# Dividing the streamed weight loads of a SwiGLU kernel at other feature tiles

**Chip, core, metric.** The kernel runs on one core of a Trainium2 chip. The metric is the device time of one execution in microseconds. The profile's span, which excludes launch work, is shorter by some 1.8 us (82.74 us against a span of 80.96 for the profiled execution of the kernel before).

## The reference

```python
# x: 32 x 32 x 512, w1 and w3: 512 x 1792, w2: 1792 x 512, all bf16
gate = einsum("bsd,df->bsf", x, w1)
up   = einsum("bsd,df->bsf", x, w3)
h    = silu(gate) * up
out  = einsum("bsf,fd->bsd", h, w2)
```

There are 1,024 rows of x, and 1,792 features are 14 "feature tiles" of 128.

## The kernel before

All weights fit on chip; the art is to start before they are there. The loads run in this order, all but two (`nc.scalar`) on the queue of SyncE:

```python
FK = 3
# ... (load_x and load_w, each one dma_start)
load_x(nc.sync, 0, 1)
load_x(nc.scalar, 1, 2)
load_w(nc.sync, w1_sb, w1_v, 0, FK, 0, 2)      # first group: tiles 0 to 2, in halves of the contraction
nc.scalar.activation(table[:], one, SIGMOID)
load_w(nc.scalar, w1_sb, w1_v, 0, FK, 2, DT)
load_w(nc.sync, w3_sb, w3_v, 0, FK, 0, 2)
load_w(nc.sync, w3_sb, w3_v, 0, FK, 2, DT)
nc.sync.dma_start_transpose(out=xT[:, :, HB:NB], in_=x_flat[HB:NB, :])
for c0, c1 in ((FK, 7), (7, 10), (10, FT)):    # three pairs of loads: w1 then w3
    load_w(nc.sync, w1_sb, w1_v, c0, c1)
    load_w(nc.sync, w3_sb, w3_v, c0, c1)
nc.sync.dma_start_transpose(out=xT[:, :, NB:N], in_=x_flat[NB:N, :])
nc.sync.dma_start(out=w2_sb[:], in_=w2_v)
```

TensorE warms up, turns the first 256 rows of x, and projects tiles 0 to 2 for those rows, then for the next 256 (its "second half"), then tiles 3 to 13 for all 512 rows:

```python
keep_warm(6, NB)                  # six matmuls on constants while x is on its way
# ... x turned; first halves of tiles 0 to 2: twelve gate, then twelve up matmuls of 256 columns
for fo in range(FK):              # second halves
    project(gates[fo], w1_sb, fo, HB, NB, range(DT), HB)
    project(ups[fo], w3_sb, fo, HB, NB, range(DT), HB)
    swiglu(gates[fo], ups[fo], fo, 0)
for nb in range(NBLK):            # two blocks of 512 rows
    for fo in range(FK if nb == 0 else 0, FT):
        # gate: four matmuls of 512 columns; up: four; then swiglu on ScalarE and VectorE
        ...
# ... then out = h w2, by 128 rows
```

Tile 3 is thus the first to need a load of the three pairs.

## Time and profile before

| | kernel before |
|---|---|
| time, median of the first 3 runs | 83.0 us (82.97 to 83.38) |
| span of the profiled execution | 80.96 us |
| TensorE busy | 94% of the span |
| VectorE / ScalarE busy | 49% / 29% |
| granted TensorE clock | 1.00 |

TensorE bounds the kernel; the prediction shows the lines. One more view of this kernel matters below, the timeline of TensorE's first group (start, length, engine, line, work, count):

```profile
4.78 1.48 PE L121 MATMUL gate_ps<-xT,w_sb 128*128 128x256 bf16 x12
6.10 1.47 PE L121 MATMUL up_ps<-xT,w_sb 128*128 128x256 bf16 x12
```

Twelve matmuls take 6.10 - 4.78 = 1.32 us from first start to next start, 0.11 us each.

### The profile page before, as it was taken

Reading aid. Unit: us, or ns where it says so; the run is one execution under the profiler, and the core shown is the slowest. Engines: PE = TensorE matmul, PEld = TensorE weight load, DVE = VectorE, ACT = ScalarE, POOL = GpSimd, SP = SyncE. Lnnn points to the kernel's source line nnn. Section 1 sums busy time; section 2 is a strip of 40 time slices with the busy share of each in tenths; the row PEclk is TensorE's granted clock in tenths of the full one; section 3 lists DMA queues with packets and bytes.
Section 4 is the critical chain, followed back from the end, with each engine's and each line's share of the span. In section 5 each row is a group of like instructions: output and inputs, shape, how many; then the busy total and the mean of one; then the engine's idle time right before and its main releaser. Section 6 shows DMA issues by size and latency. Waiting matters only on the chain.

```text
span 81.0 us, 1014 instructions
## 1 busy us (share of the span) xinstructions
PE 76.5 (94%) x382; PEld 37.4 (46%) x388; DVE 39.7 (49%) x60; ACT 23.4 (29%) x40; POOL 0.7 (1%) x6
## 2 busy tenths in 40 slices
PE   6999979999999999999999999999999999999960
PEld 2378824444444444444444444444444444444540
DVE  0040698887887887877887877873000000000010
ACT  4330742222343222343222443220220220220220
POOL 3000000000000000000000000000000000000000
DMA  1999999999992000000000000000011011011012
GB/s 10 311 284 269 349 336 344 222 67 291 350 350 64 0 0 0 0 0 0 4 8 0 0 0 0 4 0 0 15 50 65 24 41 65 29 44 65 27 41 62
DMA packets 10789, 7.67 MB, mean 95 GB/s; under 512 B 3616, under 2 KB 10784, under 8 KB 10784
## 3 DMA queue, kind: packets, MB, share of 16 engines
q1 hardware_dynamic: 10368, 7.28, 33.9%
q10 hardware_dynamic: 416, 0.33, 1.2%
q8 instruction: 3, 0.05, 0.2%
q14 instruction: 2, 0.02, 0.1%
HBM read 5.77 MB, written 1.05 MB: 84 GB/s over the span
## 4 chain that ended last, share of the span: by engine, by line
PE 82%; DMA 9%; SPq 4%; issue 1%; DVE 0%; DVEq 0%
PE o_ps L174 30%; PE up_ps L121 27%; PE gate_ps L121 26%; DMA w_sb<-in_w_dram 9%; SPq L66 2%; SPq L78 2%; SPq L62 0%; DVE o_sb L183 0%; DVEq L183 0%
## 5 line engine op out<-in xcount | busy, mean ns | idle before, releaser
L121 PEld LDWEIGHTS <-w_sb 128*128 128x128 bf16 x248 | 24.0, 98 | 25.1 <-DMA w_sb<-in_w_dram 1.5
L121 PE MATMUL up_ps<-xT,w_sb 128*128 128x512 bf16 (+1 forms) x122 | 28.7, 358 | 0.5 <-DMA w_sb<-in_w_dram 0.4
L121 PE MATMUL gate_ps<-xT,w_sb 128*128 128x512 bf16 (+1 forms) x122 | 28.7, 358 | 0.3
L131 ACT ACTIVATE sig<-gate_ps 128x512 f32<-128x512 f32 x28 | 16.7, 597 | 32.2 <-PE gate_ps L121 32.2
L174 PE MATMUL o_ps<-w_sb,hT 128*128 128x512 bf16 (+2 forms) x124 | 24.3, 355 | 0.1
L133 DVE TENSOR_TENSOR t<-gate_ps,sig 128x512 f32<-128x512 f32 x28 | 19.3, 690 | 9.0 <-ACT sig L131 8.9
L134 DVE TENSOR_TENSOR hT<-t,up_ps 128x512 bf16<-128x512 f32 x28 | 19.3, 688 | 2.9
L174 PEld LDWEIGHTS <-hT 128*128 128x128 bf16 x126 | 11.8, 98 | 12.7
L183 DVE CAST o_sb<-o_ps 128x128 bf16<-128x128 f32 x1 | 0.3, 291 | 23.0 <-PE o_ps L174 23.0
L185 ACT CAST o_sb<-o_ps 128x512 bf16<-128x512 f32 (+1 forms) x8 | 4.6, 572 | 19.6 <-PE o_ps L174 19.6
L92 PE MATMUL warm_ps<-const-bfloat16-1.0 128*128 128x512 bf16 x6 | 2.7, 623 | 0.8 <-PEq L205 0.8
L114 DVE CAST xT<-pT 128x256 bf16<-128x256 f32 (+1 forms) x3 | 1.1, 380 | 4.0 <-PE pT L104 3.9
L74 ACT ACT_TABLE_LOAD x1 | 1.3, 1283 | 1.2 <-PEq L205 1.2
L92 PEld LDWEIGHTS <-const-bfloat16-1.0 128*128 128x128 bf16 x6 | 0.7, 133 | 1.9 <-issue 1.9
L104 PEld LDWEIGHTS <-x_sb 128*128 128x128 bf16 x8 | 0.8, 135 | 1.0 <-DMA x_sb<-in_x_dram 1.0
L104 PE MATMUL pT<-ident,x_sb 128*128 128x128 bf16 x8 | 1.1, 308 | 0.1
L114 ACT CAST xT<-pT 128x128 bf16<-128x128 f32 (+1 forms) x2 | 0.6, 320 | 1.6 <-PE pT L104 1.6
masks.py:199 POOL TENSOR_SCALAR_AFFINE_SELECT ident<-ident 128x128 bf16<-128x128 bf16 x1 | 0.3, 292 | 0.1
masks.py:197 POOL MEMSET ident<- 128x128 bf16 x1 | 0.2, 204 | 0.3 <-POOLq L205 0.3
L74 ACT ACTIVATE table<-const-bfloat16-1.0 128x1 f32<-128x1 bf16 x1 | 0.2, 202 | 0.0
L205 POOL MEMSET const-bfloat16-1.0<- 128x1 bf16 x1 | 0.1, 101 | 0.0
L205 POOL MEMSET const-uint8-127<- 128x1 uint8 x1 | 0.1, 101 | 0.0
(2 smaller groups left out, 0.2 us busy)
## 6 DMA issues: line engine op xcount, KB each, us to landing
w_sb<-in_w_dram SPq DMA_DIRECT2D x4, 512.0 KB, 7.5
w_sb<-in_w_dram SPq DMA_DIRECT2D x1, 1792.0 KB, 8.6
out_dram<-o_sb SPq DMA_DIRECT2D x7, 128.0 KB, 1.7
w_sb<-in_w_dram SPq DMA_DIRECT2D x2, 384.0 KB, 7.8
w_sb<-in_w_dram SPq DMA_DIRECT2D x3, 192.0 KB, 3.9
w_sb<-in_w_dram ACTq DMA_DIRECT2D x1, 192.0 KB, 3.7
x_sb<-in_x_dram ACTq DMA_DIRECT2D x1, 128.0 KB, 3.0
x_sb<-in_x_dram SPq DMA_DIRECT2D x1, 128.0 KB, 2.8
```

What stands on the lines that cost most here:

```text
L66: queue.dma_start(out=w_sb[:, d0:d1, f0:f1], in_=w_v[:, d0:d1, f0:f1])
L74: nc.scalar.activation(table[:], one, SIGMOID)
L78: nc.sync.dma_start_transpose(out=xT[:, :, HB:NB], in_=x_flat[HB:NB, :])
L92: nc.tensor.matmul(warm_ps[:, 0:cols], lhsT=one.to_broadcast([P, P]), rhs=one.to_broadcast([P, cols]), start=True, stop=True,)
L104: nc.tensor.matmul(pT[:, i, j, :], lhsT=x_sb[:, nt, dt * P : (dt + 1) * P], rhs=ident[:], start=True, stop=True,)
L114: copy(xT[:, dts[0] : dts[-1] + 1, nts[0] * P : (nts[-1] + 1) * P], pT[:].rearrange("p d t c -> p d (t c)"),)
L121: nc.tensor.matmul(ps[:, c0 : c0 + n1 - n0], lhsT=w_sb[:, dt, fo * P : (fo + 1) * P], rhs=xT[:, dt, n0:n1], start=(dt == 0), stop=(dt == D ...
L131: nc.scalar.activation(sig[:], gate_ps[:], SIGMOID)
L133: nc.vector.tensor_mul(t[:], gate_ps[:], sig[:])
L134: nc.vector.tensor_mul(hT[:, fo, nb * NB : (nb + 1) * NB], t[:], up_ps[:])
L174: nc.tensor.matmul(o_ps[:], lhsT=hT[:, fo, nt * P : (nt + 1) * P], rhs=w2_sb[:, fo, c0 : c0 + DB], start=(fo == 0), stop=(fo == FT - 1),)
L185: nc.scalar.copy(o_sb[:], o_ps[:])
```

## The change

The intent: the first pair carries only tiles 3 to 5, so that it lands sooner; tile 6 moves to the second pair. Count, order and total bytes of the loads stay.

```diff
-    for c0, c1 in ((FK, 7), (7, 10), (10, FT)):
+    for c0, c1 in ((FK, 2 * FK), (2 * FK, 10), (10, FT)):
         load_w(nc.sync, w1_sb, w1_v, c0, c1)
         load_w(nc.sync, w3_sb, w3_v, c0, c1)
```

## The prediction

> **What bounds the kernel now.** I read four views of the kernel before, each to narrow the question. First the busy shares and the chain that ended last, to see which engine sets the end:
>
> ```profile
> PE 76.5 (94%) x382; PEld 37.4 (46%) x388; DVE 39.7 (49%) x60; ACT 23.4 (29%) x40; POOL 0.7 (1%) x6
> ...
> PE 82%; DMA 9%; SPq 4%; issue 1%; DVE 0%; DVEq 0%
> ```
>
> TensorE is busy for 94% of an 81.0 us span. It makes up 82% of the chain; one weight transfer makes up 9%. So a change of transfers is worth only what TensorE idles for them. The chain in order of time (start, length, what) shows where TensorE takes over:
>
> ```profile
> 4.64 6.89 DMA w_sb<-in_w_dram
> 11.53 0.05 issue
> 11.58 1.04 PE up_ps L121 x4
> 12.62 0.86 PE gate_ps L121 x4
> ```
>
> From 11.58 us to the last output the chain is TensorE almost without a break. What starts it is one load issued at 4.64 us that lands at 4.64 + 6.89 = 11.53 us. By the order of issue in the code this is w3 of feature tiles 3 to 6, the second load that the change touches. The timeline around that moment (start, length, engine, line, work, in brackets the idle time before):
>
> ```profile
> 9.60 0.60 PE L121 MATMUL up_ps<-xT,w_sb 128*128 128x256 bf16 x4
> ...
> 10.09 0.55 PEld L121 LDWEIGHTS <-w_sb 128*128 128x128 bf16 x4 [0.17 <-DMA w_sb<-in_w_dram]
> 10.32 0.81 PE L121 MATMUL gate_ps<-xT,w_sb 128*128 128x512 bf16 x3
> ...
> 11.57 24.50 PEld L121 LDWEIGHTS <-w_sb 128*128 128x128 bf16 x115 [0.94 <-DMA w_sb<-in_w_dram]
> 11.58 1.04 PE L121 MATMUL up_ps<-xT,w_sb 128*128 128x512 bf16 x4 [0.45 <-DMA w_sb<-in_w_dram]
> ```
>
> The bracketed numbers are not the loss: weight loads run ahead of the matmuls, and the end of a matmul is modelled. I take the loss from starts. The groups of four 256-column matmuls start at 7.41, 7.85, 8.29, 8.72, 9.16 and 9.60 us, 0.435 us apart, so tile 3's gate could have started at 9.60 + 0.435 = 10.04 us. Later groups of four 512-column matmuls start every 0.865 us (12.45, 13.31, 14.18), 0.216 us each. One of the gate's four records is missing (x3, the first shown at 10.32), so I choose to put its true start one matmul earlier, at 10.10 us, which fits the weight load at 10.09. The gate ends at 10.10 + 0.865 = 10.97 us, and the up projection starts at 11.58. **Loss at the first wait 10.10 - 10.04 = 0.06 us, at the second 11.58 - 10.97 = 0.61 us, together 0.67 us.** The sum of waits lists only three weight-load waits on these transfers (1.5 us); the third is 0.38 us before the first projection at 4.78 us and lies before anything that changes.
>
> Last, the view of the weight loads, one issue at a time (durations of the issue, then its start, then the time to landing), for the two loads that are waited for:
>
> ```profile
> L66 SPq DMA_DIRECT2D w_sb<-in_w_dram x1: 575/575/575, 4.0 to 4.0; - x1
> DMA to landing us min/median/max: 6.0/6.0/6.0
> ...
> L66 SPq DMA_DIRECT2D w_sb<-in_w_dram x1: 505/505/505, 4.6 to 4.6; - x1
> DMA to landing us min/median/max: 6.9/6.9/6.9
> ```
>
> So w1 of tiles 3 to 6 lands at 4.02 + 6.0 = 10.0 to 10.05 us, w3 at 11.53. Asked in the same way, the other four (issued at 5.19, 5.92, 6.51, 8.84) have 7.6, 8.0, 8.9 and 8.0 us to landing: w1 and w3 of tiles 7 to 9 land at 12.8 and 13.9 us, w1 and w3 of tiles 10 to 13 at 15.4 and 16.8. The spacing is 1.48, 1.27, 1.1, 1.5 and 1.4 us: about 1.45 us for 512 KB and 1.2 us for 384 KB. All six were issued by 8.84 us and the stretches from 8 to 15 us move 333 to 357 GB/s each, so a transfer lands when the bytes ahead of it have gone through; its own issue time hardly matters.
>
> **What the Trainium skill says.** "DMA: Bandwidth & Descriptors", section "Why a DMA increments its semaphore by 16 and not by 1": only the full count means that all data has landed. So tile 3, one quarter of the 512 KB, can't be used before the load of all four tiles is complete. The trace agrees: the gate's weight load starts at 10.09, right after the landing. "Perfetto Trace Analysis", section "DMA Optimizations", says that splitting transfers "may allow some to start sooner"; here the count of transfers stays and only a boundary moves, but the reason is the same. The first page's section "Specifications" asks for at least 512 B for line rate; the pieces become 3 x 128 x 2 B = 768 B instead of 1,024 B in the first pair, and the two 384 KB loads of before, whose pieces are also 768 B, took 1.27 and 1.1 us, that is 310 and 357 GB/s, against 354 for the first 512 KB, so I see no clear penalty. "TensorE: Matmul & The Clock Gate", section "Back-to-back issue gap", has 518 cycles for 512 columns (216 ns at its 2.4 GHz) beside a sustained figure of 131 ns; the trace has 216 ns, so no faster pace is to be had here and only idle time can be won.
>
> **The change part by part.** No instruction is added or removed: six loads, the same bytes, the same order, no change in the compute code. The sizes go from 512, 512, 384, 384, 512, 512 KB to 384, 384, 512, 512, 512, 512 KB.
>
> 1. w1 of the first pair carries 128 KB less. At 345 GB/s (mean of the stretch) that is 131,072 B / 345 = 0.38 us, so it lands at about 9.65 us, before TensorE wants it at 10.04. The first wait (0.06 us) goes.
> 2. w3 of the first pair has 256 KB fewer ahead of and in it: 0.76 us earlier by bytes, 11.53 - 0.76 = 10.77 us. By spacings (9.65 plus 1.1 to 1.27) it is 10.75 to 10.92 us. From landing to matmul took 0.05 us before, so the earliest start is 10.80 to 10.97. TensorE gets there at 10.04 + 0.865 = 10.90 us. So 0 to 0.07 us of wait remains, and the up projection starts at 10.90 to 10.97 instead of 11.58: 0.61 to 0.68 us gained.
> 3. Tile 6 moves into the second pair. It is wanted at 10.04 + 3 x 1.73 = 15.2 us (gate) and 16.1 us (up). Ten tile-loads of 128 KB are then done instead of eleven at w1's landing, so it lands at about 12.8 - 0.4 = 12.4 us; w3 completes the same fourteen as before and lands at 13.9. That leaves 2.8 and 2.2 us.
> 4. Tiles 10 to 13 land as before, at 15.4 and 16.8 us, and are wanted from 10.04 + 7 x 1.73 = 22.1 us on. The transposed x and w2 come behind the same bytes.
>
> Sum: 0.67 us less a remnant of some 0.05: about 0.62 us. It is all on the path, as TensorE runs without a stop from 11.58 us on. I let 0.6 stand: span 81.0 to 80.4, time 83.0 to 82.4 us.
>
> **Rivals.** (a) *The gain is eaten by VectorE or PSUM.* VectorE works almost without a pause from 8.68 to about 17.3 us on a backlog, and TensorE runs closer behind it now. If it blocked TensorE, nothing would be won: 83.0. Against it: a tile costs VectorE 0.69 + 0.69 us against 1.73 on TensorE, and with four buffers per tag, tile 4's up projection (12.63 after the change) needs tile 0's product, which ended at 10.17, 2.4 us before; that margin grows from tile to tile. I give it 3%.
> (b) *The first load does not shrink in proportion*, because of shorter pieces or because landing is mostly fixed latency. If both loads take the slower 1.27 us and w1 lands only 0.2 us earlier, w3 lands at 11.1 us; a wait of 0.25 us remains, the gain is 0.4 us and the time 82.6. Some 20%.
> (c) *The second pair becomes the wait.* It would have to slip by over 2.2 us; nothing in the steady rate speaks for that. Below 2%; then 83 or more.
> (d) *The gain drowns in the spread.* The three runs before are 82.97, 83.00 and 83.38, and the profiled one 82.74: a spread as large as the gain. The trace will show it anyway; the median may be off by 0.2.
>
> **Range and chances.** Even all idle time removed is 0.67 / 83.0 = 0.8%, so over 2% (below 81.3 us) has no source; 2% slower (above 84.7 us) needs a new wait of 1.7 us, of which I find none. The range goes from a full gain on a quick run (82.0) to almost no visible gain (82.9).
>
> **What would show it.** Right: the up projection of tile 3 starts at 10.9 to 11.0 us; no weight-load wait ahead of tile 3's gate that costs TensorE a start; no wait before tile 6 near 15.2 us; matmul pace unchanged at 0.216 us; every later start, and the end of the span, 0.6 us earlier. Wrong: w3 of the first pair landing after 11.1 us (rival b), a new gap near 15.2 or 16.1 us (c), or an early gain that is gone again before the output stage at 54.05 us (a).

## The result, and the profile after

| session | before: median, runs | after: median, runs | ratio, 95% interval |
|---|---|---|---|
| first | 83.31 us, 6 (one slow) | 81.97 us, 6 | 0.987 (0.982 to 0.992) |
| second | 82.92 us, 11 | 82.37 us, 6 | 0.993 (0.988 to 0.999) |
| third | 82.89 us, 11 | 82.15 us, 6 | 0.992 (0.987 to 0.997) |

A ratio is the mean time of one kernel's fast runs over that of the other's in the same rounds, so it is not quite the ratio of the medians quoted. The differences of the means of fast runs are 1.08, 0.60 and 0.61 us. The change is faster by 0.7 to 1.3%.

The profiled execution of the changed kernel, however, shows almost none of this: it took 82.69 us against 82.74, a span of 80.9 us against 80.96. First its busy times and its chain, by engine:

```profile
PE 77.1 (95%) x382; PEld 37.9 (47%) x388; DVE 39.5 (49%) x60; ACT 23.4 (29%) x40; POOL 0.7 (1%) x6
...
PE 95%; issue 1%; DVE 0%; DVEq 0%
```

The weight transfer (9% before) is gone from the chain: TensorE alone sets the end, from the first warming matmul on. The loads did come sooner; this is the view of the two first loads after (issue's duration and start, then time to landing):

```profile
L66 SPq DMA_DIRECT2D w_sb<-in_w_dram x1: 576/576/576, 4.0 to 4.0; - x1
DMA to landing us min/median/max: 5.4/5.4/5.4
...
L66 SPq DMA_DIRECT2D w_sb<-in_w_dram x1: 505/505/505, 4.6 to 4.6; - x1
DMA to landing us min/median/max: 6.0/6.0/6.0
```

6.0 and 6.9 us became 5.4 and 6.0 us: w1 lands at 9.4 us, w3 at 10.65 instead of 11.53. But the timeline shows TensorE coming later:

```profile
4.60 2.31 PE L121 MATMUL gate_ps<-xT,w_sb 128*128 128x256 bf16 x12
6.75 1.47 PE L121 MATMUL up_ps<-xT,w_sb 128*128 128x256 bf16 x12
...
10.24 0.60 PE L121 MATMUL up_ps<-xT,w_sb 128*128 128x256 bf16 x4
...
10.89 0.81 PE L121 MATMUL gate_ps<-xT,w_sb 128*128 128x512 bf16 x3
...
11.54 1.03 PE L121 MATMUL up_ps<-xT,w_sb 128*128 128x512 bf16 x4
```

The same twelve gate matmuls took 6.75 - 4.60 = 2.15 us instead of 1.32. Their starts in the trace are 0.213 us apart at first and 0.109 us at the end, twice the pace from some point on. Eight of the twelve were slow, so the clock was released at about 4.60 + 8 x 0.213 = 6.3 us. In the profile before it had been released by 4.78. This one accident of the execution cost 0.83 us (0.18 of it won back, as the group began at 4.60 instead of 4.78), and put TensorE at tile 3's up projection at 10.24 + 0.435 + 0.865 = 11.54 us, long after w3 was there. No idle time stands in the line at 11.54: the wait is gone, and the time it would have saved was used up ahead of it. The profile prints the granted clock as 1.00 for this execution too; the slow start is to be seen only in the pace of the matmuls.

That splits the question in two. Theory A: the change does nothing but remove TensorE's wait for w3; what that is worth differs from execution to execution. Theory B: most of the measured gain is a chance mixture of early and late clocks.

### The profile page after: what moved, and what is told of

Read it like the earlier page. It is cut to its first block, busy times and chain, and to the rows that moved or that the text cites. A ratio compares the mean times of both kernels' runs of the same rounds, so it can differ in the third digit from the quotient of the medians.

```text
span 80.9 us, 1014 instructions
## 1 busy us (share of the span) xinstructions
PE 77.1 (95%) x382; PEld 37.9 (47%) x388; DVE 39.5 (49%) x60; ACT 23.4 (29%) x40; POOL 0.7 (1%) x6
## 4 chain that ended last, share of the span: by engine, by line
PE 95%; issue 1%; DVE 0%; DVEq 0%
PE gate_ps L121 31%; PE o_ps L174 30%; PE up_ps L121 30%; PE warm_ps L92 3%; PE pT L104 1%; DVE o_sb L183 0%; DVEq L183 0%
## 5 line engine op out<-in xcount | busy, mean ns | idle before, releaser
L121 PEld LDWEIGHTS <-w_sb 128*128 128x128 bf16 x248 | 24.6, 100 | 24.6 <-DMA w_sb<-in_w_dram 0.3
L121 PE MATMUL gate_ps<-xT,w_sb 128*128 128x512 bf16 (+1 forms) x122 | 29.5, 368 | 0.2
```

The costliest lines, as they stand in the source:

```text
L121: nc.tensor.matmul(ps[:, c0 : c0 + n1 - n0], lhsT=w_sb[:, dt, fo * P : (fo + 1) * P], rhs=xT[:, dt, n0:n1], start=(dt == 0), stop=(dt == D ...
```

## The experiments

Twelve kernels ran in three further sessions of four, each beside runs of the kernel before; the second and third rows above are from the first and the last of them. One number orders all of them. From the start of tile 3's up projection TensorE runs to the end without a stop, so the span is that start plus a constant. "TensorE ready" is worked out from the starts, as in the prediction: the start of tile 2's last up group + 0.435 + 0.865 us. "Middle" and "last" are the mean of the eighth and ninth, and the last, of the sixteen part completions that the trace records for w3 of the first pair; the last one is the landing. (They are read from the semaphore events in the trace files; no view prints the middle ones.)

| execution profiled | TensorE ready | w3 middle | w3 last | up of tile 3 starts | span |
|---|---|---|---|---|---|
| before | 10.90 | 9.91 | 11.53 | 11.58 | 81.0 |
| null_before | 10.93 | 10.01 | 11.22 | 11.26 | 80.6 |
| after | 11.54 | 9.00 | 10.65 | 11.54 | 80.9 |
| same_after | 11.16 | 10.00 | 10.22 | 11.16 | 80.5 |
| after_again | 11.67 | 9.21 | 11.02 | 11.67 | 81.0 |
| w1_only | 10.54 | 9.52 | 11.39 | 11.44 | 80.8 |
| first5 | 11.13 | 11.20 | 11.67 | 11.72 | 81.1 |
| first2 | 11.53 | 9.33 | 9.50 | 11.53 | 80.9 |
| cold_before | 12.27 | 10.19 | 11.39 | 12.27 | 81.6 |
| cold_after | 12.87 | 9.30 | 10.72 | 12.87 | 82.2 |
| plain_before | 11.14 | 9.56 | 10.77 | 11.14 | 80.5 |
| plain_after | 11.35 | 9.08 | 10.16 | 11.35 | 80.7 |

In all twelve the start is the later of two times, "TensorE ready", and "w3 last" plus 0.04 to 0.05 us; and the span is the start plus 69.3 to 69.4 us. (The two probes, which move work, have another constant.)

### The two kernels again: null_before, same_after, after_again

No edit: the kernel before, and the changed kernel twice.

> The kernel before, unchanged, timed against itself, and a second profile of it. Theory A (the whole gain is TensorE's removed wait for w3 of the first pair; in the first profile it was 0.67 us, and the further 0.4 to 0.5 us of the measured gain come from executions in which that load lands later than in the profiled one): ratio 1.000 within 0.003, and in the new profile the up projection of tile 3 again starts only after w3's landing, at 11.6 to 12.1 us. Theory B (the measured gain is mostly a mixture of executions whose TensorE clock was released early or late in the first 7 us; the loads move little): ratio 1.00 but with single runs falling into two groups some 0.8 us apart, and no wait much over 0.6 us.

Measured: 82.52 us, ratio 0.997 (0.990 to 1.004). The single runs spread from 82.15 to 83.31 us, those of the kernel before beside them from 82.39 to 83.57. The timeline of this second profile of the kernel before:

```profile
9.63 0.60 PE L121 MATMUL up_ps<-xT,w_sb 128*128 128x256 bf16 x4
...
11.26 1.04 PE L121 MATMUL up_ps<-xT,w_sb 128*128 128x512 bf16 x4 [0.17 <-DMA w_sb<-in_w_dram]
```

TensorE was ready at 9.63 + 0.435 + 0.865 = 10.93 us and waited 0.33 us; w3 landed 0.31 us sooner than in the first profile. The expectation of theory A (a start of 11.6 us or later) failed in its number: the two profiles of this kernel have waits of 0.68 and 0.33 us.

> The changed kernel again, for a second profile and a tighter ratio. Theory A: ratio 0.987 to 0.992; in a profile with the clock released before the first projection (first group of gate matmuls 1.3 us from first to last start, not 2.15) tile 3's up projection starts at 10.8 to 11.0 us with no wait, span near 80.1. Theory B: ratio above 0.995 once ten more runs are in, and the spans of single runs in two groups 0.8 us apart as wide as those of the kernel before.

Measured: 82.37 us, ratio 0.993 (0.988 to 0.999), between what theory A (at most 0.992) and theory B (above 0.995) had named.

```profile
9.86 0.60 PE L121 MATMUL up_ps<-xT,w_sb 128*128 128x256 bf16 x4
...
10.51 0.81 PE L121 MATMUL gate_ps<-xT,w_sb 128*128 128x512 bf16 x3
11.16 1.03 PE L121 MATMUL up_ps<-xT,w_sb 128*128 128x512 bf16 x4
```

There is no wait at tile 3, as expected, but the start is 11.16, not 10.8 to 11.0. The clock was released in time here; instead the second halves began late, because the transposed x landed only at 7.64 us. Its span is 80.5 us, not 80.1: again the start plus the constant.

> The changed kernel a third time, for the comparison with the two-tile version on one chip and for another profile: ratio to the kernel before 0.987 to 0.994, span of the profiled run equal to the start of tile 3's up projection plus 69.4 us within 0.05 us.

Measured: 82.15 us, ratio 0.992 (0.987 to 0.997); start 11.67, span 81.0, as expected. This third profile has the latest clock of the three (2.38 us for the first twelve matmuls, from 4.49 to 6.87). What follows: the changed kernel did not wait for w3 in any of its three profiles, whatever delayed TensorE. The single runs of the changed kernel spread nearly as widely in these two sessions (81.82 to 82.86 us) as those of the kernel before (82.36 to 83.57). Theory B's two groups are half there: in the second session five runs of the kernel before lie at 82.39 to 82.63 us, five at 83.17 to 83.57 and one between, but in the third they are spread evenly, and the changed kernel's runs form no groups. In all three sessions the interval of the ratio lies below 1, so a chance mixture of clocks, theory B, is an unlikely source of the gain.

### Half the change, and the opposite: w1_only, first5

```diff
-    for c0, c1 in ((FK, 7), (7, 10), (10, FT)):
-        load_w(nc.sync, w1_sb, w1_v, c0, c1)
+    for (a0, a1), (c0, c1) in (((FK, 6), (FK, 7)), ((6, 10), (7, 10)), ((10, FT), (10, FT))):
+        load_w(nc.sync, w1_sb, w1_v, a0, a1)
         load_w(nc.sync, w3_sb, w3_v, c0, c1)
```

> Half of the change: only w1's boundary moves to 3 to 5 and 6 to 9, w3 keeps 3 to 6 and 7 to 9. w3 of the first pair then has 128 KB fewer ahead of it instead of 256 KB: it lands 0.38 us earlier instead of 0.76. Theory A: part of the gain, 0.35 to 0.45 us, ratio 0.994 to 0.996, with a wait of 0.2 to 0.4 us left ahead of tile 3's up projection. Theory B, or a gain that comes from w1's own wait (0.06 us in the trace): ratio either 1.00 or the full 0.987.

Measured: 82.50 us, ratio 0.994 (0.988 to 1.000), as theory A said; by the means it gains 0.51 us, a little more than the 0.35 to 0.45 expected. It lies between the kernel before and the changed one (0.993 on the same chip, in the same rounds) and is told apart from neither. Its profile has the earliest TensorE of all and the longest wait:

```profile
9.24 0.60 PE L121 MATMUL up_ps<-xT,w_sb 128*128 128x256 bf16 x4
...
11.44 1.04 PE L121 MATMUL up_ps<-xT,w_sb 128*128 128x512 bf16 x4 [0.66 <-DMA w_sb<-in_w_dram]
```

It was ready at 10.54 us and waited 0.90 us, not the 0.2 to 0.4 expected: w3's middle part came at 9.52 us, 0.39 us sooner than the 9.91 of the first profile, as the bytes say, but the last part lagged 1.87 us behind it.

```diff
-    for c0, c1 in ((FK, 7), (7, 10), (10, FT)):
+    for c0, c1 in ((FK, 8), (8, 11), (11, FT)):
```

> The opposite dose: the first pair covers five tiles (3 to 7), then 8 to 10, then 11 to 13. w1 lands 128 KB / 345 GB/s = 0.38 us later than in the kernel before, w3 0.76 us later. Theory A: the wait grows one for one, up projection of tile 3 at about 12.3 us, span and time 0.7 to 0.8 us longer than before, ratio 1.008 to 1.010. Theory B: ratio within 0.003 of 1.

Measured: 83.60 us, ratio 1.008 (1.001 to 1.014), one run slow; the means give 83.52 - 82.93 = 0.59 us longer.

```profile
11.72 1.04 PE L121 MATMUL up_ps<-xT,w_sb 128*128 128x512 bf16 x4 [0.42 <-DMA w_sb<-in_w_dram]
```

The sign and, nearly, the size are theory A's (0.7 to 0.8 us was expected); the interval excludes 1, though not the upper end of theory B's range (1.003). In the profile the start is 11.72 and not 12.3, since the lag was only 0.47 us in that execution, while the middle part came at 11.20 us, later by 1.29 us than in the first profile. Of that, 0.54 us was there before the pairs began: the transposing load ahead of them landed at 7.61 instead of 7.07 us. The other 0.75 us is what the bytes say.

### The landing by itself: probe_before, probe_after

Tile 3's projections are put ahead of the second halves of tiles 1 and 2; the result is the same. The second probe has the changed boundaries. The diff is shortened; the loop over the remaining tiles then begins at tile 4.

```diff
-    for fo in range(FK):
-        (second half of fo)
+    (second half of tile 0)
+    (gate, up and swiglu of tile 3)
+    for fo in range(1, FK):
+        (second half of fo)
```

> A probe of the landing by itself: boundaries of the kernel before, but tile 3's projections stand ahead of the second-half projections of tiles 1 and 2 (same work, same result), so TensorE gets to tile 3's up projection 1.74 us earlier, at about 9 us, and always waits for w3, whatever its clock did. The time is then w3's landing plus a constant. Expected: a wait of some 2.3 us ahead of tile 3's up projection, time 1.7 us over the kernel before, that is about 84.4 to 84.8 us, ratio 1.02. If the landing itself scatters from execution to execution (theory A), the single runs scatter by 0.5 us or more; if the scatter of the kernel before comes from TensorE's clock (theory B), they lie within 0.2 us.

> The same probe with the changed boundaries. The difference of the two probes is the mean shift of w3's landing over many executions. By bytes (256 KB at 345 GB/s) the load lands 0.76 us earlier: 83.7 to 84.0 us, ratio to the other probe 0.991. Theory A as first stated (landings late in unprofiled executions make the larger gain): a shift of 1.0 us or more.

Measured: 83.97 us, ratio 1.008 (1.002 to 1.014), and 83.90 us, ratio 1.008 (1.003 to 1.013). The first probe's line and then, in its own fence, the second's:

```profile
10.96 1.04 PE L121 MATMUL up_ps<-xT,w_sb 128*128 128x512 bf16 x4 [0.50 <-DMA w_sb<-in_w_dram]
```

```profile
11.04 1.04 PE L121 MATMUL up_ps<-xT,w_sb 128*128 128x512 bf16 x4 [0.27 <-DMA w_sb<-in_w_dram]
```

Neither the 1.7 us over the kernel before (the means give 0.62) nor the wait of 2.3 us came true. Without a wait TensorE would have been ready for the up projection at 9.55 and 9.18 us; part of the waiting fell ahead of the gate, which had to wait for w1 until 9.42 and 9.73 us, and w3 came earlier than in the first profile. In these two executions w3 landed at 10.91 us with the old boundaries and at 10.99 with the new. The middle parts came at 10.20 and 9.19 us, but the lags were 0.71 and 1.81 us and hid the difference. The expected shift of 0.76 us (a ratio of 0.991 between the probes) did not show: the fast runs have means of 83.78 and 83.76 us. Two of the six runs of the first probe, 84.89 and 86.36 us, count as slow and are left out, and that decides the result: with them its mean is 84.40 us. So the pair neither confirms nor measures the mean shift.

What it does show is the scatter. TensorE waits for w3 in both profiles, so the time is the landing plus a constant, and the fast runs still lie 83.59 to 84.07 and 83.14 to 84.05 us: the landing itself differs by 0.5 to 0.9 us between executions. If the two slow runs keep the constant (span minus 71.1 us in the profiled execution), w3 landed there at about 12 and 13.5 us; no trace of them was kept, and the second had a granted clock of 0.98, so that its constant may have been longer.

### TensorE late on purpose: cold_before, cold_after

```diff
-    keep_warm(6, NB)
+    keep_warm(1, NB)
```

> The kernel before with one warming matmul in place of six, so that TensorE is still at its slow pace (0.21 us for 256 columns in place of 0.11) through the first group and gets to tile 3 later than w3 lands. Theory A and B agree that the time rises, by 0.5 to 2 us. In the trace there should be no wait ahead of tile 3's up projection.

> The changed kernel with one warming matmul. If the change does nothing but bring w3 forward, it is worth nothing where TensorE comes later than w3 did before: the same time as the kernel before with one warming matmul, within 0.3 us. If it gains in some other way (issue, rate of the other loads), the 0.5 to 1 us stay.

Measured: 83.75 us, ratio 1.007 (1.000 to 1.014), one run slow; and 84.00 us, ratio 1.010 (1.005 to 1.015). The timeline of the first, then of the second:

```profile
4.57 2.74 PE L121 MATMUL gate_ps<-xT,w_sb 128*128 128x256 bf16 x12
7.11 1.84 PE L121 MATMUL up_ps<-xT,w_sb 128*128 128x256 bf16 x12
...
12.27 1.03 PE L121 MATMUL up_ps<-xT,w_sb 128*128 128x512 bf16 x4
```

```profile
4.56 2.75 PE L121 MATMUL gate_ps<-xT,w_sb 128*128 128x256 bf16 x12
7.09 2.46 PE L121 MATMUL up_ps<-xT,w_sb 128*128 128x256 bf16 x12
...
12.87 1.03 PE L121 MATMUL up_ps<-xT,w_sb 128*128 128x512 bf16 x4
```

All twelve gate matmuls are slow in both (2.54 and 2.53 us from start to start), part of the up matmuls too, and TensorE comes to tile 3's up projection at 12.27 and 12.87 us. w3 landed at 11.39 with the old boundaries, so there is no wait to remove. No gain is left: the changed kernel's mean of fast runs is 0.32 us longer (0.3 was the limit expected), and the two intervals overlap; in the two profiles the difference of 0.60 us is the later release of the clock. Within this noise, the change is worth something only where TensorE comes to tile 3 before w3 lands, and nothing by itself.

### What sets the lag: plain_before, plain_after

The result is wrong on purpose: the transposing load that stands ahead of the pairs becomes a plain load of the same bytes.

```diff
-    nc.sync.dma_start_transpose(out=xT[:, :, HB:NB], in_=x_flat[HB:NB, :])
+    x_rows = x_flat[HB:NB, :].rearrange("(p a) (b c) -> p (a b) c", a=2, b=2)
+    nc.sync.dma_start(out=xT[:, :, HB:NB], in_=x_rows)
```

> Wrong result on purpose: the transposing load of the second x half is replaced by a plain load of the same bytes into the same tile; boundaries of the kernel before. In the traces so far w3's landing is set by a few of its sixteen part completions, which come 0.04 to 1.9 us after the middle one; this lag stands from the first pair of loads on, right behind the transposing load. Theory T (the transposing load leaves some of the sixteen behind): the lag is at most 0.3 us, w3 lands at 10.0 to 10.3 us, TensorE hardly waits for it, time 82.0 to 82.4 us, ratio 0.985 to 0.992. Theory M (the lag is a matter of memory traffic, whatever load stands there): the lag stays at 0.5 us or more, w3 lands after 11 us, ratio 0.997 to 1.003.

> The same with the changed boundaries. Theory T: nothing is left to gain, time within 0.2 us of the kernel before with the plain load, since w3 now lands before 9.6 us while TensorE comes at 10.5 or later. Theory M: 0.5 us faster than that one, as in the pair under study.

Measured: 82.28 us, ratio 0.994 (0.989 to 0.999), and 82.04 us, ratio 0.991 (0.986 to 0.995). The lag stayed, 1.21 and 1.08 us, so theory T fell. Theory M named the lag rightly, but missed the first kernel's ratio (0.997 or more; 0.994 lies between the two theories) and landing (after 11 us; it was 10.77). In the second the lag stands already in both loads of w3 of the first group (1.08 and 1.13 us), and TensorE waited for the first of them:

```profile
6.38 1.48 PE L122 MATMUL up_ps<-xT,w_sb 128*128 128x256 bf16 x12 [0.42 <-DMA w_sb<-in_w_dram]
```

With the plain load the whole queue moves up, which goes with the shorter time: w3's middle part came at 9.56 instead of 9.9 to 10.2 us. By the means 0.25 us lies between the two kernels, half of theory M's 0.5 and within the intervals; whether a gain is left between them is open.

The traces also show where the lag ends. In all fourteen profiles the load that stands just ahead of a transposing load has its sixteen parts within 0.07 us of the middle one, even where the load before it lagged by 0.88 us; behind the transposing load the lag begins anew, and it is about the same for the five loads up to w1 of the third pair. It was 0.17 to 0.47 us in the three profiles whose first transposing load landed late (7.55 to 7.64 us) and 0.71 to 1.87 us in the nine where it landed at 6.78 to 7.25 us. That some of the parts fall behind is shown; why is not.

### One step further: first2

```diff
-    for c0, c1 in ((FK, 7), (7, 10), (10, FT)):
+    for c0, c1 in ((FK, 5), (5, 9), (9, FT)):
```

> One step further: the first pair covers two tiles (3 and 4), then 5 to 8, then 9 to 13. By bytes w3 lands another 0.76 us earlier, at about 9.9 us even with a lag of 1.6 us, before TensorE's earliest arrival of 10.5. Tile 5's loads would land at 11.6 and 13.1 us and are wanted at 13.5 and 14.4. If the changed kernel still waits in executions in which the clock is released early: 0.1 to 0.3 us faster than it. If not: the same within 0.15 us. If the second pair becomes the wait: slower than it, with a gap near 13.5 or 14.4 us.

Measured: 82.48 us, ratio 0.994 (0.990 to 0.998), beside 0.992 for the changed kernel in the same session.

```profile
11.53 1.03 PE L121 MATMUL up_ps<-xT,w_sb 128*128 128x512 bf16 x4
```

TensorE came at 11.53 us, w3 had landed at 9.50, and nothing waits at tile 5 either. Two tiles in the first pair buy nothing more than three, within the interval. No version with the right result beat the changed kernel.

## Why the prediction was right or wrong

**The bound, and what of the change lies on the path: right.** The time follows the start of tile 3's up projection one for one in all twelve profiles of the table, and the cold pair shows no gain where there is no wait.

**Step 1, w1's wait: right.** w1 landed at 9.4 us in the profile after (9.65 predicted), and none of the three profiles of the changed kernel waits for it at tile 3.

**Step 2, the bytes: nearly right for the middle part, too large for the landing.** Predicted was 0.76 us. The middle part of w3 came at 10.08 us in the mean of the four profiles with the old boundaries and the transposing load (9.91, 10.01, 10.20, 10.19) and at 9.34 in the five with the new (9.00, 10.00, 9.21, 9.19, 9.30): 0.74 us. The last part came at 11.26 and 10.72 us: 0.54 us. With lags of 0.2 to 1.8 us and so few executions, that mean is rough.

The middle part follows the bytes better when it is counted from the landing of the transposing load just ahead: it came 1.78 us later with two tiles in the first pair (first2), 2.22 to 2.36 with three, 2.71 in w1_only, 2.84 to 3.21 with four, 3.59 with five. That is 0.53 to 0.68 us for each 256 KB, not 0.76. The spacings of 1.27 and 1.1 us, from which the prediction and its rival (b) took their range, were landings added up from views rounded to 0.1 us; the trace has 1.19 to 1.21 us for both.

**Step 2, TensorE's side: wrong.** "TensorE gets there at 10.04 + 0.865 = 10.90 us" took one execution for all. The table has it ready from 10.54 to 11.67 us in kernels with six warming matmuls, since the clock is released somewhere between before 4.5 and 6.7 us, and a wait for x or the first weights can come on top. So the promised sign, a start at 10.9 to 11.0 us and a span 0.6 us shorter, did not appear in the profile after: start 11.54, time shorter by 0.05. The sum of 0.62 us agrees with two of the three measured differences (0.60, 0.61) and falls short of the first (1.08). It was the difference in one execution with an early clock and a late landing, and that this comes near the mean is partly luck.

**Step 3 and 4, tile 6 and later: right.** No profile after shows a wait at 15 or 16 us; w1 and w3 of the second pair landed at 12.1 and 13.7 us in the first of them.

**Rivals.** (a) was seen nowhere: in the profile after VectorE works through the same backlog and TensorE never stops for it. (b), a landing later than the bytes say, is half true, but the lag makes it, and the same lag stands with the old boundaries (0.71 to 1.62 us), so the shorter pieces are not its cause. (c) was not seen, not even in first2. (d) was right and too small: the spread of single fast runs over the three sessions, 1.2 us before and 1.0 us after, exceeds the gain, and it put the first session's median at 81.97, 0.03 us below the range's lower end, while the other two (82.37, 82.15) lie inside.

**What stays open:** why the first session gained 1.08 us, and how long the waits are that no profile caught. None of the 18 runs of the changed kernel in the three sessions took over 82.86 us; of the fast runs of the kernel before, 5 of 5, 6 of 11 and 6 of 11 did. Its two profiles (82.74 and 82.42 us) are from the quicker part. If TensorE arrives alike in both kernels, the longer runs are ones in which w3 landed later than in any kept profile of that kernel, and the mean gain is made there: spans of up to 81.8 us mean a start at 12.4 us by the constant 69.4, later than TensorE was ready in any six-warmer profile (at most 11.67). No trace of such a run exists, so this is argued and not shown. Nor is it tested that TensorE arrives alike: it was ready later in all three profiles of the changed kernel (11.16 to 11.67 us) than in both of the kernel before (10.90 and 10.93), which may be chance.

## What to carry to other kernels

When two streams meet, here TensorE's and the weights', a change to one is worth the later of the two before minus the later of the two after, and both scatter; look at several profiles of the same kernel before taking one meeting point for granted. Check the pace of the first matmuls in every profile before you compare spans: a late clock in one of them hid the whole gain here. Making the first chunk smaller still, two tiles in place of three, bought nothing measurable here, since its consumer came later than either.

## What the Trainium skill lacked or had wrong

- "TensorE: Matmul & The Clock Gate", section "What's actually happening", gives the release of the clock as varying by 500 ns either way from run to run, with a free-running window, but also counts of 6 to 14 slow matmuls for one kernel. The halved pace agrees (0.213 against 0.109 us for 256 columns), but the release fell between before 4.5 and 6.7 us in kernels with the same six warming matmuls, all begun at 0.77 to 0.78 us: more than 2 us apart.
- The same section calls the ramp's penalty under 1% of a typical span and advises against fitting a count of slow matmuls. Here it lengthened the first twelve matmuls of one profile by 0.83 us of 81 (1.0%), more than the change was worth in two of three sessions.
- The same page, section "Back-to-back issue gap", has 131 ns as the sustained figure for 512 columns; every profile here has 216 ns, its figure for the isolated case.
- "DMA: Bandwidth & Descriptors", section "Why a DMA increments its semaphore by 16 and not by 1", says that the engines finish independently but not how far apart. For w3 of the first pair the last of the sixteen came 0.17 to 1.87 us after the middle one, about the same in the next three loads of one execution, and different from execution to execution; in the load just ahead of each transposing load it was 0.07 us throughout.
